# Holding the loads of a decode-attention backward kernel to the pace of its heads, and moving its small stores to another queue

## Chip, cores and metric

One NeuronCore of one Trainium2 chip runs the program. The metric is the device time of one execution in microseconds (us), lower is better. Before: 1752.36 us, the median of 3 runs (1751.36 to 1752.77), and 1751.55 us over 15 runs when it was measured again. All runs quoted here are fast (the time within 1.5% of the fastest run of the same kernel).

## The reference, cut to what matters

The program computes one block of a transformer in decode (one token, batch 2) and all its gradients.

```python
# x [2,1,512]; k_cache, v_cache [2,32,8192,128]; wq [512,4096]; wo [4096,512]
# w1, w3 [512,1376]; w2 [1376,512]; c [2,512]; w_mod [512,3072]; all bf16
mod = silu(c) @ w_mod                                  # six vectors a batch entry
h = layernorm(x) * (1 + ca) + sa
p = softmax(q @ k_cache.T * 128**-0.5); o = p @ v_cache # 64 (batch, head) pairs
x = x + ga * (o @ wo)
x = x + gb * (silu(h2 @ w1) * (h2 @ w3)) @ w2          # h2: a second modulated layernorm
out, vjp = jax.vjp(f, ...);  return out, *vjp(grad_out) # gradients of 10 inputs
```

Each head reads K and V (2 MB each) in a first pass. The gradient of its scores needs V once more, and its gradients dK and dV (2 MB each) are written. Two heads keep their V in between, so the 64 heads read 398 MB and write 268 MB; weights and weight gradients make up the rest of 713.6 MB. There is little to compute on each byte.

## The kernel before

A scheduler written in Python puts every piece of work into a numbered slot; eight slots (NG) make one head. "A" jobs are the first pass of a head, "C" jobs its gradients. The heads of batch entry 1 are in part still in their first pass while those of entry 0 already write gradients. Two serial chains (one a batch entry) carry the small matrices from the attention output to the gradient of the attention output.

All big tiles, loads and gradients to be stored alike, share one pool of 21 buffers of 1 MB ("halves" of a head). A load is issued as soon as a buffer is free:

```python
NHALF = 21
def load_v(key, i, hf):
    t = htile()                                # one of the 21 buffers
    qd.dma_start(t[:], src_of(A_v_cache, i)[:, hf * HK:(hf + 1) * HK, :])   # qd = nc.sync
    free["half"] -= 1
...
def pump():
    while loads and free["half"] - keep[0] >= 1:   # loads: sorted by the slot that needs them
        loads.pop(0)[2]()
...
KEEP = 2                                       # buffers kept from the loads once C jobs run
...
def outer(store, dst, n, which, w2, q):        # one quarter of a head's dK or dV, on DVE
    ...                                        # takes a buffer for every half
    nc.vector.tensor_tensor(...)
    if o + QK == HK:
        sq_.dma_start(src_of(dst, n)[:, hf * HK:(hf + 1) * HK, :], t[:])   # sq_ = nc.gpsimd
        at(now[0] + 6, PL_FREE, back)          # buffer counts as free 6 slots later
```

Weight gradients are outer products, one small matmul and one copy by ACT at a time. A staging tile (`stg`, a pool of three) collects up to 512 KB, which POOL stores:

```python
def one(k):
    ...
    nc.tensor.matmul(ps[:lw, 0:rw], rsl(ln, lc, lw), rsl(rn, rc, rw), start=True, stop=True)
    nc.scalar.copy(st["t"][:lw, o:o + rw], ps[:lw, 0:rw])
    if k == len(pieces) - 1:
        dst(st["t"])                           # sq_.dma_start(out_..., st)
...
per = max(1, -(-nt // max(1, room)))           # the small tasks, per slot, after the second chain
```

## Time and profile before

| | before |
|---|---|
| time, median | 1752.36 us |
| busy share of PE / DVE / ACT | 79 / 67 / 56% |
| packets of the two main DMA queues, share of 16 engines' span | 60.1% + 39.1% |
| mean rate | 408 GB/s |

The profile page comes first. Its slices cut the span into 40 equal parts of 43.8 us; DMA is the busy share of the 16 DMA engines in tenths, GB/s what they moved. Queue q1 holds the loads that SP issues, q0 everything that POOL stores.

```profile
span 1750.1 us, 54974 instructions
...
PE 1389.5 (79%) x24112; PEld 1242.3 (71%) x24112; DVE 1169.6 (67%) x1677; ACT 980.0 (56%) x1404; POOL 393.6 (22%) x685
...
DMA  9999999999999999999999999999999999999997
GB/s 380 418 418 417 418 417 389 417 380 417 419 423 408 411 421 415 418 419 414 411 410 407 420 409 392 371 416 421 425 411 417 410 411 406 418 426 415 405 383 305
DMA packets 114846, 713.56 MB, mean 408 GB/s; under 512 B 11393, under 2 KB 20301, under 8 KB 33197
...
q1 hardware_dynamic: 73376, 425.81, 60.1%
q0 software_dynamic: 41216, 284.22, 39.1%
```

The DMA engines have no idle time to speak of until the last slice, so the kernel can only become faster by moving the same bytes at a higher rate. But for the last slice the rate swings between 371 and 426 GB/s. The packet records say what the upper end is: an 8 KB packet takes 309 ns (median), and 16 x 8192 B / 309 ns = 424 GB/s. I use 424 GB/s as the yardstick: "lost" below is the length of a stretch less the bytes moved in it divided by 424 GB/s.

The same by stages, from the view that cuts the trace into stretches. Columns: the stretch, its length, busy time (and instructions) of PE, weight loads, DVE, ACT and POOL, granted PE clock, DMA share, GB/s.

```profile
450.00:1050.00 600.00, 455.07 (x8297) 424.96 (x8295) 406.15 (x533) 307.27 (x430) 136.46 (x235) 0.83 1.01 415
1050.00:1260.00 210.00, 170.31 (x2851) 158.79 (x2849) 156.66 (x294) 126.59 (x175) 32.12 (x59) 0.69 1.00 404
1260.00:1660.00 400.00, 294.70 (x3545) 224.25 (x3545) 247.08 (x271) 240.66 (x371) 70.61 (x130) 0.59 1.01 414
...
800.00:804.00 4.00, 3.94 (x64) 3.76 (x63) 4.00 (x6) 2.29 (x3) 2.20 (x4) 0.61 1.05 422
804.00:808.00 4.00, 3.49 (x71) 2.71 (x68) 2.40 (x6) 1.48 (x3) 1.57 (x4) 1.00 0.98 326
808.00:812.00 4.00, 4.00 (x88) 4.00 (x85) 2.08 (x3) 2.62 (x3) 0.00 (x0) 1.00 1.00 422
...
1658.00:1668.00 10.00, 9.09 (x158) 8.53 (x159) 8.20 (x9) 7.33 (x11) 2.12 (x4) 0.74 0.72 291
1668.00:1700.00 32.00, 22.64 (x394) 21.38 (x392) 31.90 (x34) 19.33 (x28) 6.38 (x12) 0.73 0.96 391
1700.00:1738.00 38.00, 17.12 (x304) 16.18 (x301) 33.71 (x35) 14.38 (x20) 7.44 (x14) 0.65 0.98 399
1738.00:1744.00 6.00, 0.00 (x0) 0.00 (x0) 0.00 (x0) 0.00 (x0) 0.00 (x0) 0.50 0.26 109
```

Three things are to be seen. At 804 us the DMA engines are busy (0.98), yet move 326 GB/s: by the packet records the reads had fallen to 16 to 23 GB/s from 800 us on, came back here, and many read packets took 0.4 to 1.2 us instead of 0.31. From 1658 us no reads are left; DVE is busy all the time (31.90 of 32 us) and the stores it produces keep the DMA engines at 391 GB/s. In the last line nothing but a few DMA engines still works; from 1740 us on it is one engine alone, at 27 GB/s.

What the queues wait for. First, SP's own queue (columns: us in total, times, longest), then the group of the staging copies on ACT (its busy time and mean ns, then ACT's idle time just before them and what ended it), then the issue list (to landing: the median us in the last column).

```profile
SPq L177 <- DMA out_dram<-half: 762.0, 93, 22.1
...
SPq L177 <- PE tp L366: 80.4, 33, 11.9
```

```profile
L1213 ACT CAST stg<-m_ps 128x512 bf16<-128x512 f32 (+2 forms) x123 | 72.2, 593 | 114.3 <-DMA out_dram<-stg 86.3 <-PE m_ps L1212 24.2 <-PE s_ps L1065 3.7
```

```profile
out_dram<-stg POOLq DMA_DIRECT2D x22, 512.0 KB, 17.2
```

Loads wait for stores, since all buffers are full of early loads. One more line is POOL's at the end of the reads: start and length, then in brackets POOL's idle time before it and what ended it.

```profile
1659.47 0.52 POOL L1262 DMA_DIRECT2D out_dram<-orow  x1 [11.80 <-ACT orow L1261]
```

From 1647.7 to 1659.5 us POOL stood before a 2 KB store whose row ACT had not copied yet (the row in turn waited for DVE). DVE waited 8.2 us for a free buffer meanwhile, and from 1658 to 1668 us the rate was 291 GB/s.

### The profile page before, as it was taken

To read this page: it belongs to the slowest core of one execution; us is meant where nothing else is said; L and a number is where in the kernel's file an instruction comes from. 1 tells how busy PE (TensorE), PEld (TensorE's weight loads), DVE (VectorE), ACT (ScalarE), POOL (GpSimd) and SP (SyncE) were. 2 spreads that over 40 slices of the span, in tenths; PEclk is the share of its full clock that TensorE was granted. 3 is DMA by queue.
4 is the path that set the end of the run, shared out by engine and by line. 5 is a ranking of instruction groups with operands and counts; after the bars stand their busy time and mean duration, and the time that the engine had idled before them with its cause. 6 is when DMAs were issued, how large, how long until landed. Compare 5 with 4: busy or idle time off the path is not lost. (4 is left out here: it accounts for less than half of the span.)

```text
span 1750.1 us, 54974 instructions
## 1 busy us (share of the span) xinstructions
PE 1389.5 (79%) x24112; PEld 1242.3 (71%) x24112; DVE 1169.6 (67%) x1677; ACT 980.0 (56%) x1404; POOL 393.6 (22%) x685
## 2 busy tenths in 40 slices
PE   6999999989977777777777778788686877777673
PEld 5999998988866676776776678778554655655562
DVE  2666665867776676667667668877565576756596
ACT  4666665646544545454554555565655575765562
POOL 0333333312221222122122222111021121112121
PEclk9999999989978878888887888765655565765775
DMA  9999999999999999999999999999999999999997
GB/s 380 418 418 417 418 417 389 417 380 417 419 423 408 411 421 415 418 419 414 411 410 407 420 409 392 371 416 421 425 411 417 410 411 406 418 426 415 405 383 305
DMA packets 114846, 713.56 MB, mean 408 GB/s; under 512 B 11393, under 2 KB 20301, under 8 KB 33197
## 3 DMA queue, kind: packets, MB, share of 16 engines
q1 hardware_dynamic: 73376, 425.81, 60.1%
q0 software_dynamic: 41216, 284.22, 39.1%
q8 instruction: 188, 3.08, 0.7%
q14 instruction: 54, 0.43, 0.1%
q10 hardware_dynamic: 12, 0.01, 0.0%
HBM read 425.79 MB, written 284.20 MB: 406 GB/s over the span
## 5 line engine op out<-in xcount | busy, mean ns | idle before, releaser
L371 ACT COPY kt<-tp 128x1024 bf16<-128x1024 bf16 x768 | 775.2, 1016 | 530.2 <-PE tp L366 522.3
L366 PE MATMUL tp<-identb,half 128*128 128x128 bf16 x8192 | 779.1, 252 | 3.3 <-DMA half<-in_A_k_cache_dram 2.2
L366 PEld LDWEIGHTS <-half 128*128 128x128 bf16 x8192 | 606.0, 113 | 119.0 <-issue 113.8
L1088 DVE TENSOR_TENSOR half<-Qr,ds 128x2048 bf16<-128x2048 bf16 x256 | 309.7, 1219 | 164.5 <-DMA out_dram<-half 160.4
L1088 DVE TENSOR_TENSOR half<-DOr,e 128x2048 bf16<-128x2048 bf16 x256 | 311.1, 1215 | 106.2 <-DMA out_dram<-half 59.0
L1093 POOL DMA_DIRECT2D out_dram<-half x256 | 136.3, 532 | 969.5 <-DVE half L1088 811.8
L427 PE MATMUL m_ps<-ek,half 128*128 128x129 bf16 x4096 | 329.4, 223 | 0.2 <-DMA half<-in_A_v_cache_dram 0.2
L412 DVE TENSOR_TENSOR ek<-half,e 128x2048 bf16<-128x2048 bf16 x256 | 309.1, 1219 | 1.7 <-ACT e L404 0.8
L369 DVE COPY kt<-tp 128x1024 bf16<-128x1024 bf16 x256 | 175.7, 686 | 191.9 <-PE tp L366 186.9
L1065 PE MATMUL s_ps<-DO_bf,kt 128*128 128x1 bf16 x4096 | 192.8, 168 | 92.6 <-DVE kt L369 65.3
L1065 PEld LDWEIGHTS <-kt 128*128 128x128 bf16 x4096 | 189.7, 108 | 107.5 <-DVE kt L369 74.0
L386 PE MATMUL s_ps<-qT_bf,kt 128*128 128x1 bf16 x4096 | 177.4, 164 | 97.8 <-DVE kt L369 96.7
L427 PEld LDWEIGHTS <-half 128*128 128x128 bf16 x4096 | 249.5, 99 | 0.4 <-DMA half<-in_A_v_cache_dram 0.3
L386 PEld LDWEIGHTS <-kt 128*128 128x128 bf16 x4096 | 159.2, 98 | 102.6 <-DVE kt L369 100.9
L414 POOL COPY ek<-e 128x16 bf16<-128x16 bf16 x256 | 150.0, 606 | 326.3 <-ACT e L404 198.0
L1213 ACT CAST stg<-m_ps 128x512 bf16<-128x512 f32 (+2 forms) x123 | 72.2, 593 | 114.3 <-DMA out_dram<-stg 86.3
L1212 PE MATMUL m_ps<-half 2*128 2x512 bf16 (+2 forms) x123 | 72.4, 589 | 27.9 <-ACT stg L1213 26.4
L449 PE MATMUL k_ps<-half,pz 128*32 128x512 bf16 x1024 | 69.6, 393 | 15.6 <-POOL pz L435 15.6
L435 POOL COPY pz<-e 128x64 bf16<-128x64 bf16 x64 | 50.9, 795 | 0.0
L449 PEld LDWEIGHTS <-pz 128*32 128x32 bf16 x1024 | 21.9, 97 | 36.9 <-POOL pz L435 17.9
L416 POOL COPY E<-e 128x64 bf16<-128x64 bf16 x64 | 45.9, 717 | 0.1
L404 ACT ACTIVATE e<-s_ps,nm 128x128 bf16<-128x128 f32 x64 | 23.7, 370 | 34.0 <-DVE nm L398 34.0
(238 smaller groups left out, 738.6 us busy)
## 6 DMA issues: line engine op xcount, KB each, us to landing
out_dram<-half POOLq DMA_DIRECT2D x256, 1024.0 KB, 12.4
half<-in_A_v_cache_dram SPq DMA_DIRECT2D x252, 1024.0 KB, 12.8
half<-in_A_k_cache_dram SPq DMA_DIRECT2D x128, 1024.0 KB, 19.8
out_dram<-stg POOLq DMA_DIRECT2D x22, 512.0 KB, 17.2
half<-in_A_wq_dram SPq DMA_DIRECT2D x8, 1024.0 KB, 14.5
half<-in_w_mod_dram SPq DMA_DIRECT2D x6, 1024.0 KB, 15.4
half<-in_B_w_dram SPq DMA_DIRECT2D x6, 1024.0 KB, 14.8
half<-in_A_wo_dram SPq DMA_DIRECT2D x4, 1024.0 KB, 20.5
```

The lines of the kernel that those rows point to most:

```text
L366: nc.tensor.transpose(tp[:, j, :], block(j), identb[:])
L369: nc.vector.tensor_copy(kt[:], tp[:])
L371: nc.scalar.copy(kt[:], tp[:])
L386: nc.tensor.matmul(S_ps[i][:, cc:cc + 1], kt[:, j, :], qT_bf[:, h, b:b + 1], start=True, stop=True)
L412: nc.vector.tensor_tensor(pair(t[:, :, 0:P]), pair(K[(i, hf)][:, o:o + QK, :]), E2[i][:, ks, :].unsqueeze(2).to_broadcast((P, QK, P // 2, ...
L414: nc.gpsimd.tensor_copy(t[:, :, P:P + 1], E2[i][:, ks, 0:1])
L427: nc.tensor.matmul(m[:, 0:P + 1], vb_(i, kk), t[:, kk % QK, 0:P + 1], start=(kk == 0), stop=(kk == KK - 1), skip_group_check=True)
L449: nc.tensor.matmul(kp["ps"][NR * j:NR * (j + 1), :], pz[:, o:o + NR], K[(i, kk // HK)][:, kk % HK:kk % HK + QP, :], start=False, stop=(h = ...
L1065: nc.tensor.matmul(DP[n][:, cc:cc + 1], kt[:, j, :], DO_bf[:, b, h:h + 1], start=True, stop=True)
L1088: nc.vector.tensor_tensor(pair(t[:, o:o + QK, :]), QD[(n, which)][:].rearrange("p (a b) -> p a b", b=2).unsqueeze(1).to_broadcast((P, QK, ...
L1093: sq_.dma_start(src_of(dst, n)[:, hf * HK:(hf + 1) * HK, :], t[:])
L1212: nc.tensor.matmul(ps[:lw, 0:rw], rsl(ln, lc, lw), rsl(rn, rc, rw), start=True, stop=True)
```

## The change

Loads no longer fill every free buffer. From the first C job until six heads before the first pass ends they are issued in pairs, and only if a head needs them within two heads ("first pacing"). After the second chain they go in lots of four, with a lead that shrinks from six heads to one and a half ("late pacing"), so that reads last longer beside the stores. The first load of a lot also waits for a transpose of the current head. Besides, the small stores move from POOL to ACT's queue, weight-gradient rows are dealt out so that each partition writes 4 KB in one piece, `wq` and `w_mod` are read a second time by whole rows, and the small tasks are spread evenly over the slots.

```diff
+    pace = {"lot": 0, "lead": lambda: 0}
     def pump():
         while loads and free["half"] - keep[0] >= 1:
-            loads.pop(0)[2]()
+            need = loads[0][0]
+            if not pace["lot"]:
+                loads.pop(0)[2]()
+                continue
+            n = min(pace["lot"], len(loads))
+            if need > now[0] + pace["lead"]() or (free["half"] - keep[0] < n and need > now[0] + HG):
+                return
+            for k in range(min(n, free["half"] - keep[0])):
+                issued[0] = None
+                loads.pop(0)[2]()
+                if k == 0 and issued[0] is not None:
+                    tc.add_manual_dep(issued[0].ins, turned_last[0].ins.name, ...)
     ...
     def start_keep():
         keep[0] = KEEP
+        pace["lot"] = 2
+        pace["lead"] = lambda: 2 * NG
+    def end_pace():
+        pace["lot"] = 0
+        pump()
+    at(sA[-6], PL_FREE, end_pace)
     ...
+    gq = nc.scalar                              # all small stores: sq_ -> gq
     ...                                         # cut: row order, re-reads of wq and w_mod by rows
+    def start_lots():
+        pace["lot"] = 4
+        pace["lead"] = lambda: max(NG + NG // 2, 6 * NG - (now[0] - t1) // 2)
+    at(t1 + 24, PL_TASK, start_lots)
-    per = max(1, -(-nt // max(1, room)))        # tasks: slot t1 + 1 + k // per
+    def slot_of(k):
+        return t1 + 1 + k * room // nt
```

More of the change, by code (lines that the diff above doesn't have):

```diff
@@ L163 @@
     V = {}
+    issued = [None]
+    turned_last = [None]
     def src_of(ap, i):
@@ L170, in load_k @@
         t = htile()
-        qd.dma_start(t[:], src_of(A_k_cache, i)[:, hf * HK:(hf + 1) * HK, :])
+        issued[0] = qd.dma_start(t[:], src_of(A_k_cache, i)[:, hf * HK:(hf + 1) * HK, :])
         free["half"] -= 1
@@ L176, in load_v @@
         t = htile()
-        qd.dma_start(t[:], src_of(A_v_cache, i)[:, hf * HK:(hf + 1) * HK, :])
+        issued[0] = qd.dma_start(t[:], src_of(A_v_cache, i)[:, hf * HK:(hf + 1) * HK, :])
         free["half"] -= 1
@@ L327, in want @@
         loads.append((need, seq[0], f))
+    pace = {"lot": 0, "lead": lambda: 0}
     def pump():
         while loads and free["half"] - keep[0] >= 1:
-            loads.pop(0)[2]()
+            need = loads[0][0]
[9 more added lines that the diff above has]
+                if k == 0 and issued[0] is not None:
+                    tc.add_manual_dep(issued[0].ins, turned_last[0].ins.name,
+                                      mybir.DependencyInfo(mybir.DependencyClass.Sync, mybir.DependencyReason.DATA),
+                                      reason="loads keep pace with the heads")
     def release(n=1):
@@ L365, in transposes @@
         for j in range(GRP):
-            nc.tensor.transpose(tp[:, j, :], block(j), identb[:])
+            turned_last[0] = nc.tensor.transpose(tp[:, j, :], block(j), identb[:])
         kt = ktp.tile([P, GRP, P], BF16, name="kt", tag="kt")
@@ L1198, in row_of, with rsl, wgrad @@
             later(lambda c0=c0: part(c0))
-    def rsl(name, c0, w):
+    def rsl(name, c0, w, step=1):
         k, pb, o = rmap[name]
-        return rowst[k][pb:pb + B, o + c0:o + c0 + w]
-    def wgrad(dst, pieces, n):
+        return rowst[k][pb:pb + B, o + c0:o + c0 + (w - 1) * step + 1:step]
+    gq = nc.scalar
+    RT = 4
+    def wgrad(dst, pieces, step=1):
         st = {}
@@ L1211, in one @@
             ps = mtps()
-            nc.tensor.matmul(ps[:lw, 0:rw], rsl(ln, lc, lw), rsl(rn, rc, rw), start=True, stop=True)
+            nc.tensor.matmul(ps[:lw, 0:rw], rsl(ln, lc, lw, step), rsl(rn, rc, rw), start=True, stop=True)
             nc.scalar.copy(st["t"][:lw, o:o + rw], ps[:lw, 0:rw])
@@ L1226, with by_rows, dst @@
     row_of("d_ffn", d_ffn_bf, NC, 96)
-    for h0 in range(0, H, 4):
-        def dst(st, h0=h0):
-            sq_.dma_start(out_5.rearrange("(h p) d -> p h d", p=P)[:, h0:h0 + 4, :],
-                          st[:, 0:4 * D].rearrange("p (h d) -> p h d", h=4))
-        wgrad(dst, [("O", (h0 + k) * P, P, "d_attn", 0, D, k * D) for k in range(4)], 4)
+    def by_rows(outp, ln, rn, n):
+        for r0 in range(0, n, RT * P):
+            np_ = min(RT * P, n - r0) // RT
+            assert (n - r0) % RT == 0
+            def dst(st, r0=r0, np_=np_):
+                gq.dma_start(outp[r0:r0 + RT * np_].rearrange("(p r) d -> p (r d)", r=RT), st[:np_, 0:RT * D])
+            wgrad(dst, [(ln, r0 + k, np_, rn, 0, D, k * D) for k in range(RT)], RT)
+    by_rows(out_5, "O", "d_attn", HD)
     for outp, nm in ((out_6, "d_gate"), (out_7, "d_up")):
@@ L1235, in dst @@
             def dst(st, kc=kc, outp=outp):
-                sq_.dma_start(outp[kc * P:(kc + 1) * P, :], st[:, 0:F])
-            wgrad(dst, [("h2", kc * P, P, nm, c0, min(512, F - c0), c0) for c0 in range(0, F, 512)], 3)
-    for f0 in range(0, FC, 4):
-        nf = min(4, FC - f0)
-        def dst(st, f0=f0, nf=nf):
-            full = [f for f in range(f0, f0 + nf) if fsz(f) == P]
-            if full:
-                sq_.dma_start(out_8[f0 * P:(f0 + len(full)) * P].rearrange("(k p) d -> p k d", p=P),
-                              st[:, 0:len(full) * D].rearrange("p (k d) -> p k d", d=D))
-            if len(full) < nf:
-                k = nf - 1
-                sq_.dma_start(out_8[(f0 + k) * P:F, :], st[:FL, k * D:(k + 1) * D])
-        wgrad(dst, [("hh", (f0 + k) * P, fsz(f0 + k), "d_ffn", 0, D, k * D) for k in range(nf)], nf)
+                gq.dma_start(outp[kc * P:(kc + 1) * P, :], st[:, 0:F])
+            wgrad(dst, [("h2", kc * P, P, nm, c0, min(512, F - c0), c0) for c0 in range(0, F, 512)])
+    by_rows(out_8, "hh", "d_ffn", F)
     x2 = col("x2")
@@ L1261, in out_row @@
         nc.scalar.copy(r[:], tp[:B, 0:NC, :].rearrange("p k d -> p (k d)"))
-        sq_.dma_start(dst, r[:])
+        gq.dma_start(dst, r[:])
     def task_x2():
@@ L1273, with turned, load, tr @@
     later(task_x2)
-    wqr = {}
-    def again(w, n):
-        for pc in range(n - 1, -1, -1):
-            loads.insert(0, (0, 0, lambda pc=pc: load_piece(wqr, w, pc)))
-        pump()
-    def before_last(n, f):
-        tasks.insert(len(tasks) - n, f)
+    again = []
+    acc = {}
+    def turned(src, n, vec, name):
+        rows = {}
+        hold = {}
+        steps = [(kc, m0) for kc in range(NC) for m0 in range(0, n, GRP)]
+        assert n % GRP == 0
+        def load(kc):
+            rows[kc] = hflat()[:, 0:n * P]
+            free["half"] -= 1
+            qd.dma_start(rows[kc], src[kc * P:(kc + 1) * P, :])
+        def tr(k):
+            kc, m0 = steps[k]
+            if k == 0:
+                acc[name] = mtps()
+            tp = tps.tile([P, GRP, P], BF16, name="tp", tag="tp")
+            for j in range(GRP):
+                nc.tensor.transpose(tp[:, j, :], rows[kc][:, (m0 + j) * P:(m0 + j + 1) * P], identb[:])
+            if m0 + GRP == n:
+                rows.pop(kc)
+                release()
+                pump()
+            kt = ktp.tile([P, GRP, P], BF16, name="kt", tag="kt")
+            nc.scalar.copy(kt[:], tp[:])
+            hold[k] = kt
+        def mm(k):
+            kc, m0 = steps[k]
+            kt = hold.pop(k)
+            a = acc[name][:, 0:NC * B].rearrange("p (k b) -> p k b", b=B)
+            for j in range(GRP):
+                nc.tensor.matmul(a[:, kc, :], kt[:, j, :], vec[:, m0 + j, :],
+                                 start=(k == 0 and j == 0), stop=(m0 + j == n - 1),
+                                 skip_group_check=True)
+        for k in range(len(steps) + 1):
+            if k < len(steps) and steps[k][1] == 0:
+                again.append((len(tasks), lambda kc=steps[k][0]: load(kc)))
+            later(lambda k=k: (tr(k) if k < len(steps) else None, mm(k - 1) if k else None))
     row_of("dq", hv(DQ_bf), H, 32)
@@ L1291, in dst @@
             def dst(st, kc=kc, half=half, w=w):
-                sq_.dma_start(out_4[kc * P:(kc + 1) * P, half * w:(half + 1) * w], st[:, 0:w])
-            wgrad(dst, [("h1", kc * P, P, "dq", half * w + c0, 512, c0) for c0 in range(0, w, 512)], 4)
-    acc = {}
-    def turned(n, vec, name):
-        hold = {}
-        def tr(m0):
-            if m0 == 0:
-                acc[name] = mtps()
-            tp = tps.tile([P, GRP, P], BF16, name="tp", tag="tp")
-            for k in range(2):
-                for kc in range(NC):
-                    nc.tensor.transpose(tp[:, k * NC + kc, :],
-                                        piece(wqr, kc, m0 + k), identb[:])
-            if (m0 + 2) * P % PW == 0:
-                wqr.pop(m0 * P // PW)
-                release()
-                pump()
-            kt = ktp.tile([P, GRP, P], BF16, name="kt", tag="kt")
-            nc.scalar.copy(kt[:], tp[:])
-            hold[m0] = kt
-        def mm(m0):
-            kt = hold.pop(m0)
-            a = acc[name][:, 0:NC * B].rearrange("p (k b) -> p k b", b=B)
-            for k in range(2):
-                for kc in range(NC):
-                    nc.tensor.matmul(a[:, kc, :], kt[:, k * NC + kc, :], vec[:, m0 + k, :],
-                                     start=(m0 == 0 and k == 0 and kc == 0), stop=(m0 + k == n - 1),
-                                     skip_group_check=True)
-        later(lambda: tr(0))
-        for m0 in range(2, n, 2):
-            later(lambda m0=m0: (tr(m0), mm(m0 - 2)))
-        later(lambda: mm(n - 2))
+                gq.dma_start(out_4[kc * P:(kc + 1) * P, half * w:(half + 1) * w], st[:, 0:w])
+            wgrad(dst, [("h1", kc * P, P, "dq", half * w + c0, 512, c0) for c0 in range(0, w, 512)])
     d_h1 = col("d_h1")
@@ L1345, in task_dx0 @@
         out_row(d_x0, out_1.rearrange("b s d -> (b s) d"))
-    before_last(12, lambda: again(wq_d, HD // PW))
-    turned(H, hv(DQ_bf), "h1")
+    turned(A_wq, H, hv(DQ_bf), "h1")
     later(task_dh1)
@@ L1357, in dst @@
             def dst(st, kc=kc, m0=m0, w=w):
-                sq_.dma_start(out_10[kc * P:(kc + 1) * P, m0:m0 + w], st[:, 0:w])
-            wgrad(dst, [("sc", kc * P, P, "d_mod", m0 + c0, 512, c0) for c0 in range(0, w, 512)], 4)
-    before_last(12, lambda: again(wm_d, MD // PW))
-    turned(MC, d_mod_bf, "c")
+                gq.dma_start(out_10[kc * P:(kc + 1) * P, m0:m0 + w], st[:, 0:w])
+            wgrad(dst, [("sc", kc * P, P, "d_mod", m0 + c0, 512, c0) for c0 in range(0, w, 512)])
+    turned(w_mod, MC, d_mod_bf, "c")
     def task_dc():
@@ L1378, in chain_done @@
         pump()
+    def start_lots():
+        pace["lot"] = 4
+        pace["lead"] = lambda: max(NG + NG // 2, 6 * NG - (now[0] - t1) // 2)
     at(t1, PL_TASK, chain_done)
+    at(t1 + 24, PL_TASK, start_lots)
     nt = len(tasks)
     room = max(sC) - NG - t1 - 2
-    per = max(1, -(-nt // max(1, room)))
+    assert room > 0
+    def slot_of(k):
+        return t1 + 1 + k * room // nt
     for k, f in enumerate(tasks):
-        at(t1 + 1 + k // per, PL_TASK, f)
+        at(slot_of(k), PL_TASK, f)
+    for k, f in again:
+        want(slot_of(k) - NG, f)
+    loads.sort(key=lambda x: x[:2])
     pump()
```

## The prediction

> **What bounds the kernel now.** The DMA engines. The page shows them at 9 tenths or more in every slice but the last; the two main queues' packets take 60.1% + 39.1% of sixteen engines' span. PE (79%) and DVE (67%) have slack. An 8 KB packet takes 309 ns (median), so 16 x 8192 B / 309 ns = 424 GB/s is the ceiling (estimate; the Trainium skill, "DMA: Bandwidth & Descriptors", Specifications, gives the fabric 435 GB/s). The bytes (713.6 MB) stay, so only the distance from 424 GB/s can be won. Lost against it, by stretches:
> - 0 to 450 us, loads only: 18 us, not touched.
> - 450 to 1050 us: 13 us. Buffers are full of early loads, so the load queue waits for stores (762 us in its waits). Reads run nearly dry for 10 us, return in a lump, and for 4 us both directions make 300 to 350 GB/s, read packets taking 0.5 to 1.6 us. Such packets cost about 22 us over the run.
> - 1050 to 1130 us, second serial chain: 8 us, not aimed at.
> - 1130 to 1660 us: 10 us, with some 35 restarts of the reads.
> - From 1657 us: 30.7 MB of stores and no reads. DVE is 95 to 100% busy until 1720 us and sets 358 to 394 GB/s. 15 us go here: 3 in a hole before 1668 us, 5 for a straggling engine.
>
> **What the change does.** It holds loads to a lead of two heads, in pairs; after the second chain in fours, with a lead shrinking from six heads to one and a half. The program order puts the last load behind 245 of 256 gradient stores instead of 227. The small stores move from POOL to ACT; by the same page ("Issuing engines are not separate DMA queues") they share the same 16 engines, and their packets stay 4 KB (162 ns): nothing. The second reads of wq and w_mod (7.3 MB) change from 2 KB packets (84 ns) to 8 or 6 KB.
>
> **Worth, on the critical path (DMA):**
> - tail: the hole (3 us), and 18 stores of 1.05 MB at 424 instead of 394 GB/s (3.4 us): 6.5 us;
> - first mixed stretch: reads no longer starve, half of its slow packets go: 5 us;
> - 1130 to 1660 us: 12 lots instead of 35 restarts: 2 us;
> - larger packets: 7.3 MB at 309 instead of 336 ns per 8 KB: 1.5 us.
>
> Sum 15 us: **1737 us, 1723 to 1750 in 8 of 10 cases.** Faster by over 2% 6%, within 2% 92.5%, slower by over 2% 1.5%. Over 2% needs 35 of the 46 us lost after 450 us.
>
> **What shows it right.** Reads last until about 1700 us; the last slice but one is above 400 GB/s; the load queue waits less for stores, more for PE; read packets over 0.4 us fall from 854 to about 500; bytes equal; no long new waits on ACT.
>
> **What would make it wrong.** Lots drain before the next, adding restarts. The lead is too short, and PE waits for K and V while DMA idles. ACT now waits for an earlier load on the same semaphore before it issues a small store, and holds up its copies. After the second chain 30 stores pass with four loads: DVE binds there, and pays the tail's gain back. Or slow packets vanish: 10 us more.

## The result, and the profile after

After: 1744.33 us (median of 12 runs, 1743.16 to 1746.24) against 1751.55 us (median of 15 runs). The ratio is 0.9958, with a 95% interval of 0.9950 to 0.9966. The kernel is 7 us faster; 15 us were predicted.

The page of after, the lines that answer to those of before. Queue q10 now holds the small stores of ACT.

```profile
span 1742.9 us, 54823 instructions
...
PE 1386.9 (80%) x24113; PEld 1237.9 (71%) x24113; DVE 1171.1 (67%) x1677; ACT 983.5 (56%) x1405; POOL 366.7 (21%) x646
...
DMA  9999999999999999999999999999999999999997
GB/s 379 417 419 417 418 417 388 417 380 416 406 424 424 423 424 421 424 408 423 418 414 423 421 402 365 373 408 406 425 419 398 419 415 419 421 419 421 425 417 301
DMA packets 112954, 713.54 MB, mean 409 GB/s; under 512 B 11303, under 2 KB 20211, under 8 KB 30795
...
q1 hardware_dynamic: 70832, 425.81, 59.9%
q0 software_dynamic: 36864, 268.45, 37.0%
q10 hardware_dynamic: 5019, 15.78, 2.3%
```

The bytes agree. Slices 11 to 16 (counted from 0) now run at 421 to 424 GB/s, where before had 408 to 423. Slice 24 (365) is worse than any of before's but its last, and the last but one rose from 383 to 417.

```profile
450.00:1050.00 600.00, 457.29 (x8344) 420.64 (x8345) 412.69 (x538) 307.85 (x432) 133.45 (x236) 0.85 1.01 418
1050.00:1260.00 210.00, 165.26 (x2819) 153.75 (x2815) 154.31 (x290) 123.25 (x172) 31.64 (x58) 0.71 1.00 394
1260.00:1660.00 400.00, 309.03 (x3746) 242.98 (x3744) 268.02 (x292) 256.64 (x390) 52.31 (x99) 0.57 1.01 418
...
804.00:808.00 4.00, 2.60 (x61) 2.29 (x58) 4.00 (x6) 2.94 (x3) 0.28 (x1) 1.00 1.01 424
...
1658.00:1702.00 44.00, 24.34 (x478) 22.69 (x478) 30.40 (x34) 26.07 (x35) 6.33 (x12) 0.75 1.01 418
1702.00:1728.00 26.00, 8.48 (x136) 8.05 (x134) 18.74 (x19) 5.06 (x5) 4.29 (x9) 0.50 1.01 424
1728.00:1733.00 5.00, 0.00 (x0) 0.00 (x0) 0.00 (x0) 0.00 (x0) 0.00 (x0) 0.50 0.34 144
1733.00:1740.00 7.00, 0.00 (x0) 0.00 (x0) 0.00 (x0) 0.00 (x0) 0.00 (x0) 0.50 0.06 27
```

These are the stretches of after. The first mixed stretch and the late one are faster, the stretch of the second chain between them is slower (394 instead of 404 GB/s). The tail is at full rate until 1728 us. Then, however, 12 us pass in which most engines are done: 7 of them at 27 GB/s, which is one engine alone (one packet of 8192 B every 306 ns).

SP's queue, the staging copies and the issues of the staging tiles of after:

```profile
SPq L179 <- PE tp L383: 388.5, 37, 28.4
SPq L179 <- DMA out_dram<-half: 363.0, 52, 46.5
```

```profile
L1241 ACT CAST stg<-m_ps 128x512 bf16<-128x512 f32 (+2 forms) x124 | 72.2, 584 | 63.6 <-PE m_ps L1240 63.0 <-DMA half<-in_A_v_cache_dram 0.6
```

```profile
out_dram<-stg ACTq DMA_DIRECT2D x22, 512.0 KB, 11.0
```

SP waits half as long for stores and five times as long for PE. The staging stores land in 11.0 us, not 17.2, and ACT no longer waits for them.

Where the 7 us are, in us lost against 424 GB/s, worked out from the packet records of one traced execution each:

| stretch | before | after | after, second trace |
|---|---|---|---|
| 0 to 450 us | 17.9 | 18.0 | 17.8 |
| 450 to 1050 us (first mixed stretch) | 13.3 | 8.0 | 6.8 |
| 1050 to 1260 us (second chain) | 9.7 | 14.7 | 15.3 |
| 1260 to 1660 us | 8.9 | 6.1 | 6.9 |
| 1660 us to the end | 17.4 | 13.2 | 13.4 |
| sum | 67.2 | 60.0 | 60.3 |

The second trace comes from a later run of the same kernel. Its stretches repeat the first trace's within 1.2 us, so differences of 3 us and more between kernels are read below, smaller ones with care. A trace is also one execution only: that of e3 below took 1753.08 us, the slowest of its five runs (median 1748.72 us), that of e8 1744.75 us, the fastest (median 1746.24 us).

### The profile page after: what moved, and what is told of

The parts are those of the page before. It is cut to its first block, busy times and chain, and to the rows that moved or that the text cites. A ratio compares the mean times of both kernels' runs of the same rounds, so it can differ in the third digit from the quotient of the medians.

```text
span 1742.9 us, 54823 instructions
## 1 busy us (share of the span) xinstructions
PE 1386.9 (80%) x24113; PEld 1237.9 (71%) x24113; DVE 1171.1 (67%) x1677; ACT 983.5 (56%) x1405; POOL 366.7 (21%) x646
## 2 busy tenths in 40 slices
DMA packets 112954, 713.54 MB, mean 409 GB/s; under 512 B 11303, under 2 KB 20211, under 8 KB 30795
## 5 line engine op out<-in xcount | busy, mean ns | idle before, releaser
L383 PE MATMUL tp<-identb,half 128*128 128x128 bf16 x8192 | 767.9, 249 | 54.1 <-DMA half<-in_A_k_cache_dram 35.0
L1113 DVE TENSOR_TENSOR half<-DOr,e 128x2048 bf16<-128x2048 bf16 x256 | 311.1, 1215 | 90.6 <-DMA out_dram<-half 90.6
L1113 DVE TENSOR_TENSOR half<-Qr,ds 128x2048 bf16<-128x2048 bf16 x256 | 309.6, 1218 | 92.5 <-DMA out_dram<-half 91.4
L444 PE MATMUL m_ps<-ek,half 128*128 128x129 bf16 x4096 | 333.6, 225 | 0.3 <-DMA half<-in_A_v_cache_dram 0.3
L431 POOL COPY ek<-e 128x16 bf16<-128x16 bf16 x256 | 138.7, 560 | 330.3 <-ACT e L421 197.9
L433 POOL COPY E<-e 128x64 bf16<-128x64 bf16 x64 | 62.8, 981 | 0.1
L412 PE MATMUL s_ps<-nident,rm 128*128 128x128 bf16 x64 | 15.0, 235 | 55.4 <-DVE rm L407 55.4
L412 PEld LDWEIGHTS <-rm 128*128 128x128 bf16 x64 | 6.3, 98 | 57.5 <-DVE rm L407 57.5
## 6 DMA issues: line engine op xcount, KB each, us to landing
half<-in_A_v_cache_dram SPq DMA_DIRECT2D x252, 1024.0 KB, 19.7
```

The source lines that it names most:

```text
L383: turned_last[0] = nc.tensor.transpose(tp[:, j, :], block(j), identb[:])
L431: nc.gpsimd.tensor_copy(t[:, :, P:P + 1], E2[i][:, ks, 0:1])
L444: nc.tensor.matmul(m[:, 0:P + 1], vb_(i, kk), t[:, kk % QK, 0:P + 1], start=(kk == 0), stop=(kk == KK - 1), skip_group_check=True)
L1113: nc.vector.tensor_tensor(pair(t[:, o:o + QK, :]), QD[(n, which)][:].rearrange("p (a b) -> p a b", b=2).unsqueeze(1).to_broadcast((P, QK, ...
```

## The experiments

Twelve kernels ran, each in five rounds: e1 to e4 first, e5 to e8 second (on another chip), the others third. The kernel before ran beside each call (1750.82, 1751.33 and 1751.70 us, 9 runs each), the changed kernel only in the third. All twelve gave correct results.

| run | what it is | median us | ratio to before | 95% interval |
|---|---|---|---|---|
| e3_no_pace | changed, no pacing at all | 1748.72 | 0.9987 | 0.9974 to 1.0001 |
| e1_first_only | changed, first pacing only | 1746.62 | 0.9977 | 0.9965 to 0.9990 |
| e2_last_only | changed, late pacing only | 1746.30 | 0.9977 | 0.9964 to 0.9989 |
| e4_pool_queue | changed, small stores on POOL | 1747.09 | 0.9977 | 0.9964 to 0.9989 |
| e5_tail_sp | changed, last 11 gradient stores on SP | 1743.94 | 0.9958 | 0.9945 to 0.9970 |
| e6_no_dep | changed, no wait for a transpose | 1743.35 | 0.9957 | 0.9945 to 0.9970 |
| e7_pace_to_chain | changed, first pacing lasts longer | 1746.64 | 0.9973 | 0.9959 to 0.9987 |
| e8_lot_one | changed, lots of one load | 1746.24 | 0.9973 | 0.9961 to 0.9986 |
| a2_after_again | the changed kernel | 1744.41 | 0.9955 | 0.9942 to 0.9967 |
| e4_again | as e4_pool_queue | 1748.38 | 0.9980 | 0.9967 to 0.9992 |
| e10_pool_later | as e4, each small store two slots later | 1746.33 | 0.9969 | 0.9956 to 0.9981 |
| e9_spare_six | no pacing, six spare buffers | 1745.09 | 0.9959 | 0.9945 to 0.9972 |

An interval is about 2.2 us to each side, so a single step of 2 us is at the edge of what these rounds resolve; I lean on differences that show in several pairs.

### Each pacing alone, and none: e1, e2, e3

```diff
 e1_first_only, e3_no_pace:
-    at(t1 + 24, PL_TASK, start_lots)
 e2_last_only, e3_no_pace:
-        pace["lot"] = 2
-        pace["lead"] = lambda: 2 * NG
```

> The changed kernel without its second pacing (the lots of four after the second chain); the pairs before it stay. Theory A (the trace of after): the pairs earn 5 us before 1050 us and give them back in the second chain, whose heads and steps lie within 2 us of before; so the whole gain is made after 1260 us. Expected: 1748 to 1752 us, tail with a long stretch of stores alone as before. Theory B (as predicted): each pacing keeps what it earns: 1744 to 1747 us.

> The changed kernel without its first pacing (the pairs); the lots of four stay. Theory A: nothing is lost, 1743 to 1746 us, though the reads run dry again between 560 and 1050 us. Theory B: 5 us slower than the changed kernel, 1748 to 1750 us.

> The changed kernel without either pacing: what is left are the small stores on ACT, the new row order, the re-reads of wq and w_mod by rows, and the tasks spread evenly. Theory A and B: 1748 to 1752 us (the larger packets give 1.5 us). Rival C: the gain comes from these small edits and not from the pacing: 1743 to 1746 us.

Measured: no pacing 1748.72, first alone 1746.62, late alone 1746.30, both 1744.41 us (the last on the same chip). It was run at another time. The first pacing is worth 2.1 us without the late one and 1.9 us with it; the late one 2.4 and 2.2 us. The ratios to the kernel before, which take the drift out, say 1.8 us for either alone and 3.3 to 3.9 us for either beside the other; with intervals of 2.2 us, whether the two simply add up is open. The other edits together are worth 2.1 us (1750.82 to 1748.72), at the edge of the noise (the interval of their ratio reaches 1.0001). So the gain most likely comes from all three parts; theory C, which gave it to the small edits alone, gets a third of it. Theory A (first pacing worth nothing) and theory B (each keeps what it earns, 5 us for the first) are both wrong as stated: the first pacing keeps 2 us.

The traces show why it is 2 and not 5 or 6. Lost us by stretch:

| | no pacing | late only | first only | both |
|---|---|---|---|---|
| 450 to 1050 us | 13.6 | 13.9 | 7.0 | 8.0 |
| 1050 to 1260 us | 11.0 | 9.0 | 14.5 | 14.7 |
| 1260 us to the end | 25.5 | 20.5 | 22.5 | 19.3 |

With the first pacing 6 us less are lost before 1050 us and 3 to 6 us more in the second chain, in both pairs. (The last row of "no pacing" is on the high side, as its trace is of a slow run.)

The packet records show what moves: the slow read packets, those of 8 KB that took over 0.4 us. Their number, and in brackets their time above 309 ns, shared by 16 engines, in us:

| | before | no pacing | late only | first only | both | both (second trace) |
|---|---|---|---|---|---|---|
| 450 to 1050 us | 396 (9.9) | 497 (10.2) | 513 (10.7) | 177 (4.3) | 200 (5.0) | 166 (3.5) |
| 1050 to 1260 us | 159 (4.6) | 177 (3.8) | 164 (3.2) | 366 (8.5) | 272 (6.4) | 297 (6.5) |
| 1260 to 1660 us | 191 (4.8) | 281 (5.5) | 30 (0.6) | 226 (4.9) | 31 (0.5) | 30 (0.5) |

The first pacing takes 5 to 7 us of slow reads out of the first mixed stretch, about what that stretch gains, and 3 to 5 us of them come back in the second chain. The late pacing takes out over 4 us from 1260 to 1660 us.

The milestones of the first pass agree. The first pass's PE work was 13 us early at 687 us (674 us in e1), but only 4 us early when its last head ended (1094 to 1090 us); the chain's later steps stood at 1150 and 1216 us in before, at 1147 and 1215 us in e1. What this says of the chain is taken up under e7.

### Does the first pacing end too early? e7

```diff
-    at(sA[-6], PL_FREE, end_pace)
+    at(CS1, PL_FREE, end_pace)       # the start of the second chain
```

> The changed kernel with its first pacing ended at the start of the second chain instead of six heads before the first pass ends. The four traces so far show that the pairs save 6 us before 1050 us and lose 4 us of it between 1050 and 1260 us. Theory H, the burst of loads that refills the buffers when the pacing ends is what costs: the loss from 1050 to 1260 us falls from 14.7 to about 11 us, 1740 to 1742 us. Theory I, the chain is bound by its own steps, and what was earned before it is only idle DMA in it: 1743 to 1746 us, or slower if the weights and V come too late.

Measured: 1746.64 us, 2 us slower than the changed kernel. It was run at another time. Theory H falls: the stretch from 1050 to 1260 us lost 14.6 us as in after (14.7), without a burst at the old place. The last head of the first pass ended at 1084 us, 8 us earlier than in after, but the chain's step of 1150 us stood at 1150 us again. These are the waits from 1085 to 1155 us of that kernel; before and after show no wait for V or K in these 70 us:

```profile
PEld L383 <- DMA half<-in_A_v_cache_dram: 15.9, 2, 10.0
PE tp L383 <- DMA half<-in_A_v_cache_dram: 15.8, 2, 9.9
```

PE now waits 16 us for V of the gradient heads between the chain's steps, because the loads were held back. The time is that of theory I. Its reason, that the chain is bound by its own steps, is not shown, though, and the traces speak against its last part. Here are the 65 us up to the chain's end in before, after and the kernel without the tie (e6, below):

```profile
1150.00:1215.00 65.00, 56.04 (x778) 53.68 (x778) 45.79 (x103) 39.77 (x50) 7.98 (x15) 0.58 1.01 422
1150.00:1215.00 65.00, 56.67 (x768) 54.38 (x768) 44.97 (x103) 38.88 (x49) 7.97 (x15) 0.55 1.01 409
1150.00:1215.00 65.00, 45.22 (x896) 42.32 (x894) 50.37 (x111) 39.65 (x51) 9.57 (x18) 0.87 1.01 420
```

In before and after PE is busy for 56 of 65 us at a granted clock of 0.58 and 0.55, and the step at 1216 us is the last one. In e6 the granted clock was 0.87 and that step came at 1201 us; with 0.71 (e7) it came at 1211 us, with 0.76 (e8) at 1208 us. In the eleven traces with 0.53 to 0.59 it came at 1213 to 1218 us. So the end of the chain goes with the granted clock of that stretch. And an earlier end was worth little: the traced execution of e6, whose chain ended 15 us before that of after, was 2.2 us shorter (1742.69 and 1744.90 us), that of e8, with 8 us, 0.2 us. What slows the DMA engines of these kernels between 1050 and 1130 us is not settled: the ten traces with the first pacing's order of loads lost 9.6 to 12.2 us there, the three without any 6.6 to 8.1 us. It is slower packets in the main, the slow reads of the table above among them: the DMA share from 1050 to 1130 us is 0.99 in before and 0.98 in after. Idle engines have a part where it is lower (0.96 in the second trace of after, 0.94 in e7).

### Is it the tie to the heads, or the spare buffers? e6 and e9

```diff
 e6_no_dep:
-                if k == 0 and issued[0] is not None:
-                    tc.add_manual_dep(issued[0].ins, turned_last[0].ins.name, ...)
 e9_spare_six (no pacing):
-    KEEP = 2
+    KEEP = 6
     def end_pace():
         pace["lot"] = 0
+        keep[0] = 2
```

> The changed kernel without the wait that ties the first load of each lot to a transpose; the order of the loads and stores is unchanged. Theory F, the order and the spare buffers are what counts: 1743 to 1746 us, and the load queue waits for stores no more than now (391 us). Theory G, without the wait the loads run ahead into the spare buffers and starve the stores: 1746 to 1750 us, reads run dry between 560 and 1050 us again, loss there 11 us or more instead of 8.

> No pacing at all, but six buffers instead of two are kept from the loads until six heads before the first pass ends. Theory N, spare buffers for the stores are what the first pacing gives: the loss from 450 to 1050 us falls from 13.6 (no pacing) to about 8 us, the reads do not run dry, and the time is that of the first pacing alone, 1745 to 1748 us. Theory O, it takes the tie to the heads: loss 12 to 14 us, reads run dry, 1748 to 1750 us.

Measured: without the tie 1743.35 us; with nothing but six spare buffers 1745.09 us, which is 0.7 us from the changed kernel and 3.6 us faster than no pacing (same chip). In both, the loss from 450 to 1050 us fell to the level of the pacing: 7.6 and 8.4 us, and the reads did not run dry before 900 us (in steps of 2 us they never fell below 130 GB/s, in before below 40 GB/s in 12 of 225 steps). The trace of the spare-buffer kernel in stretches:

```profile
450.00:900.00 450.00, 350.21 (x6457) 318.25 (x6455) 319.86 (x420) 237.06 (x333) 103.78 (x185) 0.88 1.01 423
900.00:1050.00 150.00, 104.57 (x1871) 98.42 (x1869) 91.34 (x118) 71.08 (x100) 29.43 (x51) 0.78 0.99 403
```

It runs at 423 GB/s for 450 us, one short of the yardstick, and gives some back where the spare buffers are released. Theories F and N hold in this: spare buffers alone do what the first pacing does, and the wait for a transpose adds nothing that these rounds show. A side result corrects my reading of before. This is SP's queue in the kernel without the tie:

```profile
SPq L179 <- DMA out_dram<-half: 667.6, 82, 45.6
```

SP waits for stores nearly as long as in before (762 us), and yet its reads never ran dry in that stretch. Its figure missed what I expected under either theory (391 us or less, or starvation with it). The length of that wait was no measure of the harm; whether the reads run dry is.

### Do the lots matter? e8

```diff
-        pace["lot"] = 2
+        pace["lot"] = 1
-        pace["lot"] = 4
+        pace["lot"] = 1
```

> The changed kernel with the same leads, but loads issued one by one in both pacings. Theory J, the lead counts and the lots do not: 1743 to 1746 us. Theory K (predicted), the lots count because a read that restarts meets slow packets: more restarts after 1260 us (15 read stretches become 30 or more), slow read packets over 646, and 1746 to 1749 us.

Measured: 1746.24 us, some 2 us slower than lots of two and four, at the low end of theory K. From 1260 to 1660 us the reads came in 16 pieces (a pause of over 0.5 us ends a piece), against 11 in both traces of after. But slow read packets were 684, against 646 and 633 in the two traces of after, and between 1260 and 1660 us they cost 0.4 us of the engines' time in this kernel and 0.5 in after. So lots may help a little, and not by way of slow reads there. How is open, and the size is at the edge of what the intervals allow; the trace cannot tell, since its execution took 1744.75 us, no longer than that of after (1744.90 us).

### The queue of the small stores: e4, e4 again, e10

```diff
 e4_pool_queue, e4_again, e10_pool_later:
-    gq = nc.scalar
+    gq = nc.gpsimd
 e10_pool_later:
-                dst(st["t"])
+                at(now[0] + 2, PL_TASK, lambda t=st["t"]: dst(t))
```

> The changed kernel with its small stores back on POOL, pacing kept. If the queue is worth nothing, as predicted: within 1.5 us of 1744. If waits of ACT on landings of earlier loads cost something: faster, 1740 to 1742 us. If the stores on POOL hold up gradient stores behind them: slower, 1747 to 1752 us.

> The changed kernel itself once more, on the chip of the next three, for a comparison with them and for a second trace. 1743 to 1746 us. The loss from 450 to 1050 us again near 8 us and from 1050 to 1260 us near 14 us if those figures belong to the kernel and not to the one execution.

> The changed kernel with its small stores on POOL, repeated beside the changed kernel. If the difference of 2.8 us was real: 2 to 4 us slower than the changed kernel of these rounds; if it was chance: within 1 us.

> Small stores on POOL, each issued two slots later than its last copy, so that POOL does not wait for ACT before it issues the gradient stores behind it (35 us of such waits with the stores on POOL). Theory L, POOL's order is the cost: 1743 to 1745 us, like the queue of ACT. Theory M, the small stores share a ring with the gradient stores, land late (18 to 20 us instead of 11) and keep their three buffers, for which ACT waits 103 us: no better than the small stores on POOL as they were, 1746 to 1749 us.

Measured: 1747.09 us; beside each other, 1744.41 us on ACT's queue and 1748.38 us on POOL's. The queue is worth 4 us there, with the pacings in place, and it was predicted to be worth nothing. Issued two slots later on POOL: 1746.33 us, in the middle. The staging copies and the issues of the repeated kernel on POOL:

```profile
L1241 ACT CAST stg<-m_ps 128x512 bf16<-128x512 f32 (+2 forms) x124 | 72.2, 590 | 123.7 <-DMA out_dram<-stg 100.4 <-PE m_ps L1240 14.1 <-PE s_ps L1090 4.7
```

```profile
out_dram<-stg POOLq DMA_DIRECT2D x22, 512.0 KB, 19.7
```

On POOL's queue the staging stores take 19.7 us to land instead of 11 us and ACT waits 100.4 us for their tiles; from 1260 to 1660 us 11.1 us are lost against 6.9 us in the trace of the changed kernel beside it. In e10 they landed in 16.3 us, ACT waited 116.2 us, and the time improved by 2 us, so the length of ACT's wait is no measure of the harm. Theory M would fit what is left in e10, theory L (POOL's order) the other half; the two halves are each about as large as the intervals, so only their sum is firm. All kernels move the same bytes with the same engines. Two ways in which a second queue can help are thus on the table: 512 KB no longer stand behind several stores of 1 MB, and stores of 1 MB no longer wait on POOL behind a small one that is not ready. A third was not tested: ACT's queue is a hardware queue and POOL's a software one, and no run put the small stores on SP or on a second software queue.

For the second way before's profile has a direct case, the 11.8 us before the row's store. With the small stores on ACT's queue and no late pacing (e3, e1) the stretch from 1658 to 1668 us ran at 414 and 408 GB/s instead of 291; with the pacings and the stores back on POOL it ran at 358, 315 and 338 GB/s (e4, e4 again, e10), in after at 423. In before alone the reads had ended by then, so this is a sign and no proof.

### The engine that ends last: e5

```diff
+            stores[0] += 1
-            sq_.dma_start(
+            (nc.sync if stores[0] > 245 else sq_).dma_start(
```

> The changed kernel with its last 11 gradient stores issued by SP (hardware queue) instead of POOL (software queue). In the trace of the changed kernel 14 or 15 of the 16 engines finish their last store by about 1731 us and one works on alone at 27 GB/s until 1740 us, 4 to 5 stores behind; where the tail is bound by DVE (before, first pacing alone) it is only 2 behind, and 5 us. Theory D, the lag belongs to the software queue's ring on that engine: the lone stretch shrinks to under 4 us, 1738 to 1741 us. Theory E, that engine has had more work or slower packets whatever the queue: the lone stretch stays at 8 to 12 us, 1743 to 1746 us.

Measured: 1743.94 us, ratio 0.9958, the same as the changed kernel's. The stretches of its end:

```profile
1702.00:1726.00 24.00, 6.67 (x128) 6.29 (x125) 18.50 (x19) 4.97 (x5) 0.00 (x0) 0.64 1.01 425
1726.00:1733.00 7.00, 0.00 (x0) 0.00 (x0) 0.00 (x0) 0.00 (x0) 0.00 (x0) 0.50 0.53 226
1733.00:1740.00 7.00, 0.00 (x0) 0.00 (x0) 0.00 (x0) 0.00 (x0) 0.00 (x0) 0.50 0.10 41
```

The engines now spread out more (226 and 41 GB/s where after had 144 and 27), and one works alone only from 1736 us on, but it ends at 1740.6 us as in after (1739.9 us). By the time theory E holds; its 8 to 12 us alone do not. The queue of the last stores does not decide when the slowest engine ends. Which engine it is, and why it lags, stays open: the packet records at hand do not name engines.

The lag goes with the shape of the tail, though. For comparison the tail of the kernel with the first pacing alone, whose reads end at 1671 us:

```profile
1672.00:1736.00 64.00, 39.59 (x790) 36.09 (x790) 56.95 (x61) 39.74 (x53) 12.05 (x23) 0.82 0.97 395
1736.00:1742.00 6.00, 0.00 (x0) 0.00 (x0) 0.00 (x0) 0.00 (x0) 0.00 (x0) 0.50 0.21 87
```

| | MB after the last read | rate falls below 200 GB/s | last store's packet | between |
|---|---|---|---|---|
| before | 31.5 | 1740 us | 1744.4 us | 4 us |
| no pacing (e3) | 26.0 | 1742 us | 1748.0 us | 6 us |
| first only (e1) | 26.3 | 1737 us | 1741.8 us | 5 us |
| late only (e2) | 12.3 | 1731 us | 1741.5 us | 11 us |
| both (after) | 12.5 | 1729 us | 1739.9 us | 11 us |
| both (second trace) | 12.2 | 1729 us | 1740.1 us | 11 us |

Where DVE holds the stores at 395 GB/s for 60 us and more, the slow engine is only 4 to 6 us behind at the end. That it catches up in the engines' idle moments is how I explain it; no run takes the lag away. Where the engines are full until the last store, it works on for 11 us after the rate has fallen.

### Nothing beats the changed kernel clearly

Removing the tie (e6, 1743.35 us) and storing the last gradients from SP (e5, 1743.94 us) are no slower than the changed kernel, and simpler in e6's case, but no faster beyond the interval. Six spare buffers with the late pacing were not tried together.

## Why the prediction was right or wrong

The time lay inside the range (1744.33 in 1723 to 1750) and the class (within 2%) was the likely one. The centre was 7 us too low: 15 us were summed up and 7 came. There is luck in it. The range ended 2 us short of the time of before, so nearly any gain lay inside, and 3 to 4 of the 7 us came from the small stores' queue, which was put down as nothing: with these stores on POOL, the change was worth 3.7 and 3.3 us (e4 and e4 again). Term by term:

- **What bounds the kernel: right.** The bytes are equal (713.56 and 713.54 MB), and the rate is what changed; the us lost against 424 GB/s fell from 67.2 to 60.0, as they must with equal bytes.
- **First mixed stretch, 5 us: right in place, wrong in worth.** The reads no longer starve, slices 11 to 16 run at 421 to 424 GB/s, and 5.3 to 6.5 us less are lost before 1050 us. Half of its slow read packets went, as predicted (396 to 200 and 166). But 5 us more are lost in the second chain, and on/off tests give 2 us (up to 3.9 by the ratios). The step that failed is to count the 5 us as "on the critical path", as if the stretches after it stayed as they were: from 1050 to 1260 us slow read packets rose from 159 to 272 and 297, and 14.7 and 15.3 us were lost instead of 9.7. That the chain itself binds is not shown: in the trace of e6 it ended 15 us earlier, and the execution was 2.2 us shorter. What slows the packets there stays open. My prediction called this chain "not aimed at" and left it at that. The cause I named was half right: full buffers, yes (e9), but the 762 us of SP's waits were no sign of it (e6).
- **Tail, 6.5 us: mis-sized, and the step that failed is the "straggling engine", which I took as 5 us in both kernels.** The reads last until 1701 us, the hole is gone and the rate is 424 GB/s until 1728 us, all as predicted. But in a full tail that engine works on for 11 us instead of 4, which takes back most of what "18 stores at 424 instead of 394 GB/s" (3.4 us) gave. Net, the tail lost 17.4 us before and 13.2 us after. The late pacing has no part in that net: with it the tails lost 13.2 to 13.6 us (after, its second trace and e2), without it 12.0 and 13.8 us (e1 and e3). The hole went with the other edits: it was gone without the late pacing, and in part back with the small stores on POOL.
- **1130 to 1660 us, 2 us from fewer restarts: size right, and the traces fit the mechanism.** The late pacing is worth 2.2 to 2.4 us, and 1260 to 1660 us lost 10.5 and 11.7 us without it against 6.1 and 6.9 us with it. By the same count of pieces as above the reads came in 33 and 30 pieces without it (e1, e3) and in 9 to 11 with it, and slow reads cost 4.9 and 5.5 us against 0.5 to 0.6. So the stretch gained over 4 us, of which a tail at full rate gave part back. It need not be the lots: lots of one load had as few slow reads and yet cost 2 us.
- **Larger packets, 1.5 us: not separated.** They are part of the 2.1 us of e3.
- **The small stores' queue, nothing: wrong.** Beside the pacings it is worth 4.0 us. The premise (same 16 engines, no more bandwidth) was right; the conclusion left out two things: the three staging tiles, which come free only when a store lands, and POOL's order. Before's own profile had the signs: 86.3 us of ACT waiting for staging stores, and 11.8 us of POOL waiting for one row while gradient stores stood behind it. The parts overlap: all other edits with the queue give 2.1 us without pacing.
- **Slow read packets, from 854 to about 500: too hopeful.** 646 and 633: those of the second chain rose, as said above.
- **Fears:** no wait of ACT for an earlier load appeared. PE's waits for K before its transposes did rise, from 2.2 to 35.0 us over the run, nearly all in the first mixed stretch and at most 4.2 us each; the DMA share there stayed at 1.01, so the engines did not idle for them. In e7, where the pacing lasted longer, PE waited for V between the chain's steps. After the second chain a slice fell to 398 GB/s, as feared, though others beside it rose to 419.

## What to carry to other kernels

When DMA is busy all the time, cost a change by stretches against the rate of its best packets, and then ask what the next stretch does with a gain: here 5 us won before the second chain were lost again during it, and a tail at full rate left one of the sixteen engines 11 us of work. Loads that fill every free buffer can make the total rate worse by starving first the stores and then themselves; a few buffers kept from the loads did as well here as tying loads to the work. A second queue added no bandwidth here, but small stores landed on it in 11 us instead of 16 to 20, and large stores did not wait for a small one that was not ready.

## What the Trainium skill lacked or had wrong

- "DMA: Bandwidth & Descriptors", section "Issuing engines are not separate DMA queues", says that several issuing engines only save "the time on the sequencer it takes to initiate the DMA". Its premise agrees with the runs (equal bytes, no slice above 426 GB/s with either queue). The conclusion was too narrow here: small stores on ACT's queue landed in 11.0 us, on POOL's beside 1 MB stores in 16.3 to 19.7 us, and the kernel was 4.0 us faster (beside each other on one chip). POOL's sequencer may account for about half of that (e10). The same page's section "Queues, rings and completion order" has what could explain the landing times (each engine "round-robins between the queue rows it has work for"), but draws no advice from it; no run here isolates it.
- The same page, section "Specifications", gives the fabric 435 GB/s. The median 8 KB packet gives 424 GB/s, and a stretch of 26 us with stores alone ran at 424 GB/s.
- No page says that reads coming back after they had nearly stopped beside stores run slow: 326 GB/s for 4 us at a busy share of 0.98, with many read packets of 0.4 to 1.2 us instead of 0.31 us. Why is not settled here either. Over the runs such packets cost 0.5 us (31 of them, after) to 5.5 us (281, e3) between 1260 and 1660 us.
- The same page, section "Latency and other measured facts", says that engines 7 and 15 are usually slower and guesses at the software queue's rings. Here one engine worked on for 11 us after the rate had fallen below 200 GB/s, and ended no earlier when the last 11 stores came from a hardware queue (1740.6 and 1739.9 us). Earlier stores were on the software queue still, and no run here shows which engine it is.
